# Fourier, expert and rational stages on one core: weight pairs scaled through PSUM, a sine stage that accumulates both signs, and a Nyquist row brought in by DMA

## Chip, cores and metric

The kernel runs on one core of a Trainium2 chip. The metric is device time in microseconds (us), the median of several runs. The profile is one further execution, taken with the hardware profiler.

## What is computed

The reference chains three parts. The first takes the real part of a two-dimensional Fourier transform of `x` (8 batches, 3072 x 256, float32), the second sends every one of the 24576 rows to one of eight experts, the third is a layer with a rational activation:

```python
X = np.fft.fft(x, axis=1)
X = np.fft.fft(X, axis=2)
x = X.real                                    # 24576 rows of 256
e = argmax(x @ w_gate);  g = softmax(x @ w_gate)[e]
x = g * (relu(x @ w1[e]) @ w2[e])             # w1[e] 256x1024, w2[e] 1024x256
h = x @ w_in                                  # 256x2048
g = (a0 + a1*h + a2*h**2 + a3*h**3) / (1 + |b0|*|h| + |b1|*h**2 + 1e-6)
out = g @ w_out                               # 2048x256
```

## The kernel before

The program has a Fourier part (the first eighth of the time) and an expert and rational part (the rest). The change lies in the Fourier part alone.

The Fourier part runs a loop of steps `s`, one for each batch `b` and half `jh` of the first transform's outputs: 16 steps and a last pass. Every engine takes its instructions in the order in which the loop body writes them, so the order in the body is the order on each queue. A step works on several things at once.

- **Folding** (VectorE, DVE). `fold_a`, `fold_b` and `fold_c` combine the rows of batch `b + 1` by symmetry, half of them in each step, into the operands `eo`. When `fold_c` has read its half of `xh`, SyncE (SP) issues `load_x`, 1.5 MB for the batch after (L254). That happens in steps 0 to 11, since the later steps have no further batch to load.
- **First transform** (TensorE, PE). `stage1` (L426) does one of four products of the step (even and odd, cosine and sine): three or six float32 matmuls with 384 columns into a PSUM bank of the pool `psA`. ScalarE (ACT) moves the result to the tiles `u[0]` to `u[3]`. The sine products have 127 rows, so row 127 of `u[1]` and `u[3]` is unused.
- **Second transform** (PE, ACT, DVE) of the step before. `second(p, g)` for g = 0, 1, 2 calls `stage2`, which makes two blocks of 128 rows. A block takes three matmuls of 137 columns, 129 of the transform and 8 gate logits: the cosine part (L442), the Nyquist row `u128` through a matmul with 8 rows (L443), and the sine part, which has its own columns (L445). ACT copies the cosine part to `pp` (L448), and DVE makes sum and difference into the output rows `y`, forward and mirrored, and into the logits `L` (L451 to L456).
- **Gate.** `choose` (DVE) finds the expert of a row, `gate_rank` (PE, L492 to L497) counts the rows of each expert two steps later, `gate_b` inside `finish` (DVE, L509 to L537) turns counts into addresses, and `send` scatters the rows: 12 indirect DMAs a step, issued by GpSimd (POOL, L541). `second_norm` (ACT, L484) sums squares of the rows.
- **Weight jobs.** The 16 weight matrices `w1[e]`, `w2[e]` (1 MB each, 128 x 2048 float32) become pairs of float16, a high half and the rest, scaled by a power of two, and go to `ws` in DRAM. One job runs per step, spread over two steps: `job_load` (SP, L558 and L561), `job_square` (ACT, L568), `job_sum` (PE, L572, inside `gate_rank`), `job_factor` (DVE, inside `gate_b`), `job_scale` (ACT, L589, in place), `job_split` (high half by ACT, L593; the rest by POOL, L594), `job_store` (SP, L598, one step on). A job has two buffers `wf` for the loaded matrix and two buffers `wh` for the pair. The load of the next matrix waits until L594 has read the old one.

SP's queue in a step of before is: load, store, then `load_x`. At the top of step 15 it also takes two 1 MB loads of `w_in`. All these go through the one hardware DMA queue of SP.

PSUM holds three banks for `psA`, two double banks for `psB` (`pq` of `stage2`) and one bank for everything small (`psS`).

Of the kernel before, what the change touches and what calls it, by code (L numbers as in the profile page):

```python
# [20 lines left out]
P = 128  # L21
S = 3072
# [13 lines left out]
def shape_constants():  # L36
# [23 lines left out]
    c["c_rs"] = np.sin(v * (((m[:, None] + 1) * k2[None, :]) % D)).astype(np.float32)  # L60
# [4 lines left out]
    c["c_lg"] = np.ascontiguousarray(np.concatenate([cf, sf, alt], 2)).astype(np.float32)  # L65
    r8 = np.ones((8, 145), np.float32)
    r8[:, :129] = (-1.0) ** k2
    r8[:, 137:] = np.eye(8)
# [55 lines left out]
def fourier_moe_rational_kernel(ctx, tc, xl, wg, w1, w2, w_in, w_out, av, bv, cst, out):  # L124
# [90 lines left out]
    with ExitStack() as c1:  # L215
# [23 lines left out]
        rc, rs, onesf = carve(0, 137), carve(0, 137), carve(0, P)  # L239
# [4 lines left out]
        r8 = carve(1, 145)[0:8]  # L244
# [16 lines left out]
        lg = spare[0][:, 0:528].rearrange("p (t c) -> p t c", t=2)  # L261
# [17 lines left out]
        nc.sync.dma_start(out=rs[:, 0:129], in_=cst["c_rs"])  # L279
# [83 lines left out]
        def edge_logits():  # L363

            pl = psS.tile([P, 512], F32, tag="ss", name="pl")
            for t in range(2):
                nc.tensor.matmul(pl[:, 0:8], lhsT=lg[:, t, 0:128], rhs=wgt[:, t], start=t == 0, stop=t == 1)
            for t in range(2):
                nc.tensor.matmul(pl[:, 8:16], lhsT=lg[:, t, 128:256], rhs=wgt[:, t], start=t == 0, stop=t == 1)
            for t in range(2):  # L370
                nc.tensor.matmul(pl[0:8, 16:24], lhsT=lg[:, t, 256:264], rhs=wgt[:, t], start=t == 0, stop=t == 1)
            V.tensor_copy(out=rc[:, 129:137], in_=pl[:, 0:8])
            V.tensor_copy(out=rs[:, 129:137], in_=pl[:, 8:16])
            al = fp.tile([8, 8], F32, name="al")
            V.tensor_copy(out=al, in_=pl[0:8, 16:24])
            V.tensor_tensor(out=r8[:, 129:137], in0=r8[:, 129:137], in1=al, op=ALU.mult)
# [57 lines left out]
        def stage2(b, jh, u, g, y, L, rb):  # L434

            pq = psB.tile([P, 2, 512], F32, tag="s2", name="pq")
            for k in range(2):
                par, q = divmod(2 * g + k, 3)
                ueu, uou = u[2 * par], u[2 * par + 1]
                js = slice(q * 128, q * 128 + 128)  # L440
                jg = jh * NH + q * 128
# [7 lines left out]
            La, Lm = L[:, 4 * g:4 * g + 2], L[:, 4 * g + 2:4 * g + 4]  # L449
            ya, ym = y[:, 0:2], y[:, 2:4]  # L450
            V.tensor_tensor(out=La, in0=pp[:, :, 129:137], in1=pq[:, :, 385:393], op=ALU.subtract)  # L451
            V.tensor_tensor(out=Lm, in0=pp[:, :, 129:137], in1=pq[:, :, 385:393], op=ALU.add)
            V.tensor_tensor(out=ya[:, :, 0:129], in0=pp[:, :, 0:129], in1=pq[:, :, 256:385], op=ALU.subtract)
            V.tensor_tensor(out=ym[:, :, 0:129], in0=pp[:, :, 0:129], in1=pq[:, :, 256:385], op=ALU.add)
            V.tensor_tensor(out=ya[:, :, 255:128:-1], in0=pp[:, :, 1:128], in1=pq[:, :, 257:384], op=ALU.add)
            V.tensor_tensor(out=ym[:, :, 255:128:-1], in0=pp[:, :, 1:128], in1=pq[:, :, 257:384], op=ALU.subtract)  # L456
# [29 lines left out]
        def gate_rank(key, nt, sums=()):  # L486
# [12 lines left out]
            for i, n in enumerate(sums):  # L499
                job_sum(n, pr[:, 144 + i:145 + i], start=False, skip_group_check=True)  # L500
            gst[key] += (pr,)

        def gate_b(key, ys_, nt, big, idsrc, idoff, sums=()):
# [8 lines left out]
            for i, n in enumerate(sums):  # L512
                job_factor(n, pr[:, 144 + i:145 + i])
# [57 lines left out]
        def job_sum(n, dst, **kw):  # L571
            nc.tensor.matmul(dst, lhsT=onesf, rhs=J[n][2], stop=True, **kw)  # L572

# [12 lines left out]
        def job_scale(n):  # L586
            e, which = jobs[n]
            wf = J[n][0]
# [19 lines left out]
        def job_alone(n):  # L608
            pa = psS.tile([P, 512], F32, tag="ss", name="pa")
            job_sum(n, pa[:, 0:1], start=True)  # L610
            job_factor(n, pa[:, 0:1])

# [8 lines left out]
        U, Y, LL, NQ, RB = {}, {}, {}, {}, {}  # L621

        def second(s, g):
            b, jh = steps[s]
# [6 lines left out]
            stage2(b, jh, U[s], g, y, LL[s], RB[b])  # L631

        def batch_row(b):
            RB[b] = gp.tile([8, 137], F32, tag="rb", name="rb")
            V.tensor_scalar(out=RB[b], in0=r8[:, 0:137], scalar1=r8[:, 137 + b:138 + b], scalar2=None, op0=ALU.mult)
# [7 lines left out]
        def finish(s, sums=()):  # L643
            b, jh = steps[s]
            sli, gt = gate_b(s, Y[s], 12, None if jh else bigm[:, 0:12], ids[:, jh], b * S, sums)
            top_norm(NQ.pop(s), gt, 12)
            return Y.pop(s), sli
# [39 lines left out]
        for s in range(NS + 1):  # L687
# [4 lines left out]
            for n in new:  # L692
                job_load(n)
            for n in old:
                job_store(n)
            old = now
# [3 lines left out]
            if on:  # L700
# [4 lines left out]
                if s and jh == 0:  # L705
                    batch_row(b)
                stage1(b, jh, eo, 0, u)
            if s == 0:
                stage1(b, jh, eo, 2, u)
                job_square(0)  # L710
                edge_logits()
                batch_row(0)
            if 2 <= s < NS:
                second_norm(s - 2, 2)
            if fold:
                fold_a(b + 1, jh)
            if s and s != NS - 1:
                second(p, 0)
            if 2 <= s < NS:
                gate_rank(s - 2, 12, now)  # L720
                send(*finish(s - 2, now))
# [3 lines left out]
            if s and on:  # L725
                stage1(b, jh, eo, 1, u)
            if s:
# [11 lines left out]
            for n in now:  # L739
                if s == 1:  # L740
                    job_square(n)
                    job_alone(n)
                job_scale(n)
            if s == 0:
                edge_col(0, 0)
                edge_col(0, 1)
                job_alone(0)
# [4 lines left out]
            if fold:  # L752
                fold_c(b + 1, jh, nxt)
            if s:
                second(p, 2)
                second_norm(p, 1)
                if on:
                    choose(p)
            for n in now:
                job_split(n, nc.gpsimd if s != NS - 2 else V)  # L760
            if on:
                stage1(b, jh, eo, 3, u)
            if s == NS - 1:
# [7 lines left out]
            if s == 0:  # L771
                job_scale(0)
                job_split(0)
                job_store(0)
            else:
                for n in new:
                    job_square(n)
            if on and jh == 1:
                eo = nxt
        for n in old:  # L780
            job_store(n)
# [589 lines left out]
```

## Time and profile before

| | |
|---|---|
| median of 3 runs | 3660.04 us (3654.47 to 3663.76) |
| profiled execution | 3663.37 us, of which the span from first to last instruction is 3661.3 us |
| mean granted TensorE clock | 0.978 of full speed |
| PE matmul busy over the span | 3498.4 us (96%) |
| DVE, ACT, POOL busy over the span | 3085.3, 3176.3, 3059.6 us |

The profile gives, for the one core, busy time by engine, groups of equal instructions by source line, the instructions in order of time with what ended the idle time ahead of them, and the chain of work that ended last. Times in a view count from the first instruction. The shares over the whole span are dominated by the expert and rational part, so the Fourier part has to be read from its own stretches.

### The profile page before, as it was taken

How to read it: one execution, taken by the hardware profiler on the slowest of the kernel's cores; microseconds unless marked ns; L12 is line 12 of the kernel's file. 1: busy time of each engine (PE TensorE's matmuls, PEld its weight loads, DVE VectorE, ACT ScalarE, POOL GpSimd, SP SyncE). 2: the span in 40 equal slices, each digit the busy share in tenths (PEclk: the TensorE clock that was granted, in tenths of full speed). 3: DMA queues.
4: the chain of work that ended last, by engine and by line, in shares of the span. 5: the costliest groups of instructions: out<-in, count | busy, mean ns of one | idle time of the engine just before them, and what ended most of it. 6: DMA issues, size and time to landing. Idle time of an engine off the chain costs nothing.

```text
span 3661.3 us, 76234 instructions
## 1 busy us (share of the span) xinstructions
PE 3498.4 (96%) x30136; PEld 3014.4 (82%) x30136; DVE 3085.3 (84%) x3531; ACT 3176.3 (87%) x4082; POOL 3059.6 (84%) x2874
## 2 busy tenths in 40 slices
PE   6999588999999999999999999999999999999996
PEld 3665377888888888888888888888888888888885
DVE  6888566888888888888888888888888888888887
ACT  3666346999999999999999999999999999999997
POOL 3777566888888888888888888888888888888886
PEclk9899689999999999999999999999999999999999
DMA  6666452521133111511151113222332113321210
GB/s 251 216 230 198 166 142 45 90 44 41 45 64 68 45 41 41 90 43 42 43 89 45 39 43 70 60 45 42 67 67 44 39 43 70 61 45 42 45 33 18
DMA packets 342823, 270.16 MB, mean 74 GB/s; under 512 B 180382, under 2 KB 317606, under 8 KB 335152
## 3 DMA queue, kind: packets, MB, share of 16 engines
q1 hardware_dynamic: 309440, 185.32, 20.7%
q0 software_dynamic: 33024, 79.96, 8.9%
q8 instruction: 236, 3.87, 0.6%
q14 instruction: 123, 1.01, 0.1%
HBM read 329.07 MB, written 96.92 MB: 116 GB/s over the span
## 4 chain that ended last, share of the span: by engine, by line
POOL 39%; ACT 27%; issue 14%; PE 13%; DVE 5%; DMA 1%; another core or an unknown queue 1%; POOLq 0%; SPq 0%; DVEq 0%; ACTq 0%
POOL glo L1210 12%; POOL bnd L1141 5%; POOL out_dram L1235 5%; ACT ghi L1209 5%; ACT hhi L1084 4%; PE ps L426 4%; ACT h L1198 3%; POOL wslot L856 3%; ACT L L1196 3%; POOL xr L1035 2%; PE po L1222 1%; POOL xp L1036 1%; PE h L1064 1%; PE h L1067 1%; PE pq L445 1%
## 5 line engine op out<-in xcount | busy, mean ns | idle before, releaser
L1064 PE MATMUL h<-yr,win 128*128 128x256 f16 x3072 | 753.9, 273 | 4.7 <-DVE u__48257 L1201 2.0
L1065 PE MATMUL h<-yr,win 128*128 128x256 f16 x3072 | 753.9, 273 | 0.0
L1222 PE MATMUL po<-wout,ghi 128*128 128x256 f16 x6144 | 733.6, 273 | 12.8 <-ACT ghi L1209 8.8
L1222 PEld LDWEIGHTS <-ghi 128*128 128x128 f16 x6144 | 600.5, 98 | 84.2 <-ACT ghi L1209 13.8
L1067 PE MATMUL h<-yr,win 128*128 128x256 f16 x3072 | 586.4, 273 | 0.0
L1198 ACT ACTIVATE h<-L,bnd 128x1024 f32<-128x1024 f32 x385 | 429.7, 1116 | 41.2 <-DVE u__48756 L1189 1.6
L1064 PE MATMUL h<-xt,wslot 128*128 128x256 f16 x1648 | 407.6, 274 | 12.4 <-DVE hlo L1090 5.7
L1065 PE MATMUL h<-xt,wslot 128*128 128x256 f16 x1648 | 407.8, 274 | 0.0
L1222 PE MATMUL po<-wout,glo 128*128 128x256 f16 x3072 | 398.5, 273 | 2.5 <-POOL glo L1210 2.4
L1064 PE MATMUL py<-hhi,wslot 128*128 128x256 f16 x1648 | 377.8, 276 | 6.1 <-ACT hhi L1084 4.7
L1065 PEld LDWEIGHTS <-wslot 128*128 128x128 f16 x3296 | 324.6, 98 | 71.6 <-issue 33.5
L1065 PE MATMUL py<-hhi,wslot 128*128 128x256 f16 x1648 | 377.6, 276 | 0.0
L1064 PEld LDWEIGHTS <-wslot 128*128 128x128 f16 x3296 | 324.9, 99 | 47.9 <-issue 5.9
L1067 PEld LDWEIGHTS <-wslot 128*128 128x128 f16 x3296 | 324.2, 98 | 42.3 <-issue 3.0
L1222 PEld LDWEIGHTS <-glo 128*128 128x128 bf16 x3072 | 300.1, 98 | 38.8 <-POOL glo L1210 4.1
L1065 PEld LDWEIGHTS <-win 128*128 128x128 f16 x3072 | 300.6, 98 | 38.0 <-issue 3.2
L1064 PEld LDWEIGHTS <-win 128*128 128x128 f16 x3072 | 300.6, 98 | 37.0 <-DVE u__48257 L1201 2.3
L1067 PEld LDWEIGHTS <-win 128*128 128x128 f16 x3072 | 300.6, 98 | 34.7
L1067 PE MATMUL h<-xt,wslot 128*128 128x256 f16 x1648 | 317.0, 274 | 0.0
L541 POOL DMA_INDIRECT xs<-y,sli x192 | 214.6, 1118 | 85.9 <-issue 49.5
L1090 DVE SCALAR_TENSOR_TENSOR hlo<-h,hhi 128x1024 f16<-128x1024 f32 x197 | 239.9, 1218 | 22.5 <-ACT hhi L1084 16.0
L1235 POOL DMA_INDIRECT out_dram<-o,id x192 | 199.2, 1037 | 53.0 <-issue 44.6
(4922 smaller groups left out, 9583.8 us busy)
## 6 DMA issues: line engine op xcount, KB each, us to landing
xr<-xs SPq DMA_DIRECT2D x103, 258.0 KB
ys<-yw SPq DMA_DIRECT2D x103, 256.0 KB
yr<-ys SPq DMA_DIRECT2D x96, 256.0 KB
xh<-x_l SPq DMA_DIRECT2D x14, 1536.0 KB
wf<-in_moe_w_dram SPq DMA_DIRECT2D x16, 1024.0 KB
ws<-wh SPq DMA_DIRECT2D x16, 1024.0 KB
wslot<-ws SPq DMA_DIRECT2D x4, 1024.0 KB
xh<-x_l SPq DMA_DIRECT2D x4, 768.0 KB
```

Source lines behind the costliest of these rows:

```text
L426: nc.tensor.matmul(ps[0:m, 0:n], lhsT=lhsT, rhs=mat[:, c, 0:n], start=c == 0, stop=c == nk - 1)
L541: ins = nc.gpsimd.indirect_dma_start(out=xs, out_offset=bass.IndirectOffsetOnAxis(ap=sli[:, t0 + t:t0 + t + 1], axis=0), in_=y[:, t], in_o ...
L1064: nc.tensor.matmul(ps, lhsT=wa[i], rhs=xa[i], start=i == 0, stop=False)
L1065: nc.tensor.matmul(ps, lhsT=wb[i], rhs=xa[i], start=False, stop=False)
L1067: nc.tensor.matmul(ps, lhsT=wa[i], rhs=xb[i], start=False, stop=i == n - 1)
L1090: V.scalar_tensor_tensor(out=hlo[:, sl], in0=ps, scalar=0.0, in1=hhi[:, sl], op0=ALU.max, op1=ALU.subtract)
L1141: nc.gpsimd.tensor_scalar(out=out, in0=in0, scalar1=a, scalar2=b, op0=op0, op1=op1)
L1198: nc.scalar.activation(out=ps, in_=L, func=AF.Exp, scale=-1.0, bias=st["bnd", j][3])
L1209: nc.scalar.activation(out=ghi, in_=w_, func=AF.Copy)
L1210: (V if fs[0] else nc.gpsimd).tensor_tensor(out=glo, in0=w_, in1=ghi, op=ALU.subtract)
L1222: nc.tensor.matmul(ps[:, q], lhsT=g[:, f - fs[0], q * P:(q + 1) * P], rhs=wout[:, h, 4 * u + f], start=g is ghi and u == 0 and f == 0 and ...
L1235: ins = nc.gpsimd.indirect_dma_start(out=out, out_offset=bass.IndirectOffsetOnAxis(ap=t[:, q:q + 1], axis=0), in_=o[:, q], in_offset=None, ...
```

## The change

What each engine does for a weight job is new. ACT makes the high half straight from the loaded matrix with the scale (`job_half`), and scales the matrix once more in four quarters of 512 columns, each into one PSUM bank of a new pool `psW` (`job_full`). DVE subtracts the high half from the bank (`job_rest`). POOL has no part in it any more, and the matrix is no longer overwritten. Bank `psW` is single and is also where `job_sum` puts its column, so the quarters and the sum take turns in it. `psA` gives one bank up for it.

The pieces are spread over two steps. The squares of a job move from the end of the step in which its load was issued to the top of the next step, behind `stage1(0)`. The sum moves out of `gate_rank` to behind `stage1(1)`. Half and quarter 0 come after `second(p, 1)`, quarter 1 after `second(p, 2)`, quarter 2 at the end of the step, quarter 3 in the next step behind `second(p, 0)`. The store, and behind it the load of the next matrix, move from the top of the step to behind `finish`.

In `stage2` a block takes two matmuls of 274 columns in place of three of 137: the cosine part against the constants twice over, and the sine part against minus and plus the constants, summed in PSUM. Row 127 of the sine constants holds the alternating signs of the Nyquist row, and row 127 of `u[1]` and `u[3]` gets the Nyquist row itself: `column_row` issues two DMAs of 1.5 KB (SP) at the end of each step, from `u128` into the tiles. DVE and ACT then only copy: ACT the forward part of both signs in one instruction, DVE the logits and the two mirrored parts. `batch_row` and `pp` go away.

```diff
-    c["c_rs"] = np.sin(v * (((m[:, None] + 1) * k2[None, :]) % D)).astype(np.float32)
+    rs = np.sin(v * (((m[:, None] + 1) * k2[None, :]) % D))
+    rs = np.stack([-rs, rs], 1)
+    rs[127] = (-1.0) ** k2
+    c["c_rs"] = rs.astype(np.float32)
...
-        psA = c1.enter_context(tc.tile_pool(name="psA", bufs=3, space=PSUM))
+        psA = c1.enter_context(tc.tile_pool(name="psA", bufs=2, space=PSUM))
...
+        psW = c1.enter_context(tc.tile_pool(name="psW", bufs=1, space=PSUM))
...
-        def stage2(b, jh, u, g, y, L, rb):
+        def column_row(b, jh, u):
+
+            for par in range(2):
+                nc.sync.dma_start(out=u[2 * par + 1][P - 1:P], in_=u128[b:b + 1, par, jh * NH:jh * NH + NH])
+
+        def stage2(u, g, y, L):
...
-                nc.tensor.matmul(pq[:, k, 0:137], lhsT=ueu[:, js], rhs=rc, start=True, stop=False)
-                nc.tensor.matmul(pq[:, k, 0:137], lhsT=u128[0:B, par, jg:jg + 128], rhs=rb[0:B],
-                                 start=False, stop=True)
-                nc.tensor.matmul(pq[:, k, 256:393], lhsT=uou[0:P - 1, js], rhs=rs[0:P - 1],
-                                 start=True, stop=True)
-            pp = gp.tile([P, 2, 137], F32, tag="pp", name="pp")
-            nc.scalar.activation(out=pp, in_=pq[:, :, 0:137], func=AF.Copy)
...
+                nc.tensor.matmul(pq[:, k, 0:274], lhsT=u[2 * par][:, js],
+                                 rhs=rc.unsqueeze(1).to_broadcast([P, 2, 137]), start=True, stop=False)
+                nc.tensor.matmul(pq[:, k, 0:274], lhsT=u[2 * par + 1][:, js],
+                                 rhs=rs.rearrange("p s c -> p (s c)"), start=False, stop=True)
+            p4 = pq[:, :, 0:274].rearrange("p k (s c) -> p s k c", s=2)
+            y4 = y.rearrange("p (s k) d -> p s k d", s=2)
+            nc.scalar.activation(out=y4[:, :, :, 0:129], in_=p4[:, :, :, 0:129], func=AF.Copy)
+            V.tensor_copy(out=L[:, 4 * g:4 * g + 4].rearrange("p (s k) e -> p s k e", s=2), in_=p4[:, :, :, 129:137])
+            for s_ in range(2):
+                V.tensor_copy(out=y4[:, s_, :, 255:128:-1], in_=p4[:, 1 - s_, :, 1:128])
...
+        def job_sum(n):
+
+            pw = psW.tile([P, 512], F32, tag="w", name="pw")
+            nc.tensor.matmul(pw[:, 0:1], lhsT=onesf, rhs=J[n][2], start=True, stop=True)
+            job_factor(n, pw[:, 0:1])
...
-            nc.scalar.activation(out=wf, in_=wf, func=AF.Copy, scale=(s1c, s2c)[which][:, e:e + 1])
-
-        def job_split(n, engine=nc.gpsimd):
-            wf, wh, _ = J[n]
-            nc.scalar.activation(out=wh[:, 0], in_=wf, func=AF.Copy)
-            engine.tensor_tensor(out=wh[:, 1], in0=wf, in1=wh[:, 0], op=ALU.subtract)
...
+        def job_half(n):
+            wf, wh, sc = job_scaled(n)
+            nc.scalar.activation(out=wh[:, 0], in_=wf, func=AF.Copy, scale=sc)
+
+        def job_full(n, k):
+
+            wf, _, sc = job_scaled(n)
+            pw = psW.tile([P, 512], F32, tag="w", name="pw")
+            nc.scalar.activation(out=pw, in_=wf[:, 512 * k:512 * k + 512], func=AF.Copy, scale=sc)
+            J[n].append(pw)
+
+        def job_rest(n, k):
+
+            wh, pw = J[n][1], J[n][3 + k]
+            c = slice(512 * k, 512 * k + 512)
+            V.tensor_tensor(out=wh[:, 1, c], in0=pw, in1=wh[:, 0, c], op=ALU.subtract)
```

The loop body of a step (0 < s < 15) is then, in order, with the moved or new calls marked by +:

```
  stage1(0)   + job_square(now)   second_norm(s-2, 2)   fold_a   + job_rest(old, 2)
  second(p, 0)   + job_full(old, 3)   gate_rank(s-2)   send(finish(s-2))
+ job_rest(old, 3)   + job_store(old)   + job_load(new)
  stage1(1)   + job_sum(now)   second(p, 1)   second_norm(p, 0)   fold_b
+ job_half(now)   + job_full(now, 0)   stage1(2)   fold_c with load_x   + job_rest(now, 0)
  second(p, 2)   second_norm(p, 1)   + job_full(now, 1)   choose(p)   + job_rest(now, 1)
  stage1(3)   + column_row   + job_full(now, 2)
```

In step 15 quarters 2 and 3 and the store follow at once at the end, and in step 0 job 0 does its half, its four quarters and its store there.

## Rows read from the trace of the kernel before

**Rows 1.** Busy time by stretch: busy and count for PE, PEld, DVE, ACT, POOL, then clock, DMA share, GB/s.

```profile
123.00:354.00 231.00, 212.40 (x981) 137.57 (x981) 197.89 (x569) 153.18 (x396) 179.04 (x131) 0.91 0.68 223
460.00:3661.00 3201.00, 3136.61 (x28510) 2784.83 (x28510) 2738.82 (x2514) 2926.70 (x3431) 2760.73 (x2648) 0.99 0.26 54
```

**Rows 2.** POOL in order of time: start, duration, instruction, idle time before and its end.

```profile
109.30 4.10 POOL L594 TENSOR_TENSOR wh<-wf,wh 128x2048 f16<-128x2048 f32 x1
...
222.85 4.09 POOL L594 TENSOR_TENSOR wh<-wf,wh 128x2048 f16<-128x2048 f32 x1
...
228.87 0.99 POOL L541 DMA_INDIRECT xs<-y,sli  x1 [1.94 <-DVE y L529]
...
358.89 4.08 POOL L594 TENSOR_TENSOR wh<-wf,wh 128x2048 f16<-128x2048 f32 x1
```

**Rows 3.** DVE in order of time around the same POOL instruction.

```profile
222.95 4.11 DVE L514 TENSOR_TENSOR pos<-pos,o 128x96 f32<-128x96 f32 x1
227.09 0.25 DVE L516 TENSOR_REDUCE sl<-pos 128x12 f32<-128x96 f32 x1
...
229.18 0.17 DVE L537 TENSOR_TENSOR nrm<-nq,nrm 128x12 f32<-128x12 f32 x1
```

**Rows 4.** Groups by form, 80 to 420 us: busy, mean ns, idle before and its releasers.

```profile
L541 POOL DMA_INDIRECT xs<-y,sli x173 | 194.4, 1123 | 76.3 <-issue 44.0 <-DVE y L529 27.7 <-DVE ee L329 1.5
L484 ACT ACTIVATE sq<-y 128x256 bf16<-128x256 f32 x176 | 73.1, 416 | 7.7 <-DVE y L455 3.6
...
L594 POOL TENSOR_TENSOR wh<-wf,wh 128x2048 f16<-128x2048 f32 x14 | 58.3, 4164 | 32.5 <-ACT wh L593 20.7 <-issue 11.7
...
L448 ACT ACTIVATE pp<-pq 128x274 f32<-128x274 f32 x44 | 17.3, 393 | 46.3 <-PE pq L445 32.4 <-remote 8.4 <-issue 2.9
...
L589 ACT ACTIVATE wf<-wf,s1c 128x2048 f32<-128x2048 f32 x7 | 13.9, 1987 | 0.0
...
L325 DVE TENSOR_TENSOR xh<-xh 128x384 f32<-128x384 f32 x6 | 3.3, 548 | 0.0
```

**Rows 5.** PE in order of time, the matmuls that bound steps and blocks.

```profile
81.03 0.40 PE L442 MATMUL pq<-wslot,u 128*128 128x137 f32 x2
...
242.35 0.59 PE L572 MATMUL pr<-part,wslot 128*128 128x1 f32 x2 [4.00 <-issue]
...
267.12 0.46 PE L492 MATMUL pr<-o,tri 128*128 128x88 f16 x11
...
286.25 0.46 PE L492 MATMUL pr<-o,tri 128*128 128x88 f16 x11
...
291.34 4.04 PE L426 MATMUL ps<-wslot,oo 128*128 128x384 f32 x12
295.21 0.40 PE L442 MATMUL pq<-wslot,u 128*128 128x137 f32 x2
...
297.39 3.07 PE L426 MATMUL ps<-so,oo 128*127 128x384 f32 x9
...
304.51 0.40 PE L442 MATMUL pq<-wslot,u 128*128 128x137 f32 x2
```

**Rows 6.** SP's DMA issues of one step, in order of time.

```profile
226.96 0.38 SPq L561 DMA_DIRECT2D wf<-in_moe_w_dram  x1
227.38 0.58 SPq L598 DMA_DIRECT2D ws<-wh  x1
233.54 0.32 SPq L254 DMA_DIRECT2D xh<-x_l  x1
```

**Rows 7.** Busy time in stretches of 2 us in that step, columns as in Rows 1.

```profile
234.00:236.00 2.00, 2.00 (x9) 1.24 (x7) 2.00 (x8) 1.17 (x3) 1.50 (x2) 1.00 1.13 416
...
242.00:244.00 2.00, 1.65 (x4) 1.26 (x5) 0.00 (x0) 1.94 (x9) 1.70 (x2) 0.50 0.73 272
244.00:246.00 2.00, 2.00 (x4) 1.01 (x3) 0.98 (x5) 1.12 (x6) 1.68 (x3) 0.50 0.26 91
```

**Rows 8.** Chain that ended last, behind the first loads of the expert part: start, us, what.

```profile
462.42 10.89 DMA ab<-in_moe_a_dram
```

More of the change, by code (lines that the diff above doesn't have):

```diff
@@ L64, in shape_constants @@
     alt = np.repeat(((-1.0) ** kk)[:, None], 8, 1).reshape(2, 128, 8).transpose(1, 0, 2)
-    c["c_lg"] = np.ascontiguousarray(np.concatenate([cf, sf, alt], 2)).astype(np.float32)
-    r8 = np.ones((8, 145), np.float32)
+    sa, sb = -sf, sf.copy()
+    sa[:, :, 127] = sb[:, :, 127] = alt[:, :, 0]
+    c["c_lg"] = np.ascontiguousarray(np.concatenate([cf, sa, sb, alt], 2)).astype(np.float32)
+    r8 = np.ones((8, 137), np.float32)
     r8[:, :129] = (-1.0) ** k2
-    r8[:, 137:] = np.eye(8)
     c["c_r8"] = r8
@@ L367, in edge_logits @@
                 nc.tensor.matmul(pl[:, 0:8], lhsT=lg[:, t, 0:128], rhs=wgt[:, t], start=t == 0, stop=t == 1)
+            for s_ in range(2):
+                for t in range(2):
+                    nc.tensor.matmul(pl[:, 8 + 8 * s_:16 + 8 * s_], lhsT=lg[:, t, 128 + 128 * s_:256 + 128 * s_],
+                                     rhs=wgt[:, t], start=t == 0, stop=t == 1)
             for t in range(2):
-                nc.tensor.matmul(pl[:, 8:16], lhsT=lg[:, t, 128:256], rhs=wgt[:, t], start=t == 0, stop=t == 1)
-            for t in range(2):
-                nc.tensor.matmul(pl[0:8, 16:24], lhsT=lg[:, t, 256:264], rhs=wgt[:, t], start=t == 0, stop=t == 1)
+                nc.tensor.matmul(pl[0:8, 24:32], lhsT=lg[:, t, 384:392], rhs=wgt[:, t], start=t == 0, stop=t == 1)
             V.tensor_copy(out=rc[:, 129:137], in_=pl[:, 0:8])
-            V.tensor_copy(out=rs[:, 129:137], in_=pl[:, 8:16])
+            V.tensor_copy(out=rs[:, :, 129:137], in_=pl[:, 8:24].rearrange("p (s c) -> p s c", s=2))
             al = fp.tile([8, 8], F32, name="al")
-            V.tensor_copy(out=al, in_=pl[0:8, 16:24])
+            V.tensor_copy(out=al, in_=pl[0:8, 24:32])
             V.tensor_tensor(out=r8[:, 129:137], in0=r8[:, 129:137], in1=al, op=ALU.mult)
@@ L484, in norms, with gate_rank @@
                 nc.scalar.activation(out=sq, in_=y[:, t, 0:D], func=AF.Square, accum_out=nq[:, t:t + 1])
-        def gate_rank(key, nt, sums=()):
+        def gate_rank(key, nt):
             sh, o1 = gst[key]
@@ L498, in gate_rank, with gate_b @@
                                  stop=t == nt - 1, skip_group_check=True)
-            for i, n in enumerate(sums):
-                job_sum(n, pr[:, 144 + i:145 + i], start=False, skip_group_check=True)
             gst[key] += (pr,)
-        def gate_b(key, ys_, nt, big, idsrc, idoff, sums=()):
+        def gate_b(key, ys_, nt, big, idsrc, idoff):
             sh, o1, pr = gst.pop(key)
@@ L606, in jobs_of @@
             return range(min(NJB, 1 + per * s), min(NJB, 1 + per * (s + 1)))
[L608 to L611, printed above, removed]
         edge_rows()
@@ L630, in second @@
             Y[s].append(y)
[L631 to L635, printed above, removed]
+            stage2(U[s], g, y, LL[s])
         def second_norm(s, g):
@@ L641, in choose, with finish @@
             gate_a(s, LL.pop(s), 12, None if steps[s][1] else msk[:, 0:12])
-        def finish(s, sums=()):
+        def finish(s):
             b, jh = steps[s]
-            sli, gt = gate_b(s, Y[s], 12, None if jh else bigm[:, 0:12], ids[:, jh], b * S, sums)
+            sli, gt = gate_b(s, Y[s], 12, None if jh else bigm[:, 0:12], ids[:, jh], b * S)
             top_norm(NQ.pop(s), gt, 12)
@@ L691, in fourier_moe_rational_kernel @@
             new = jobs_of(s) if on else ()
[L692 to L696, printed above, removed]
             if s == NS - 1:
@@ L704, in fourier_moe_rational_kernel @@
                 u = U[s] = {}
-                if s and jh == 0:
-                    batch_row(b)
                 stage1(b, jh, eo, 0, u)
+            for n in now:
+                job_square(n)
             if s == 0:
@@ L716, in fourier_moe_rational_kernel @@
                 fold_a(b + 1, jh)
+            for n in old:
+                job_rest(n, 2)
             if s and s != NS - 1:
                 second(p, 0)
+            for n in old:
+                job_full(n, 3)
             if 2 <= s < NS:
-                gate_rank(s - 2, 12, now)
-                send(*finish(s - 2, now))
+                gate_rank(s - 2, 12)
+                send(*finish(s - 2))
+            for n in old:
+                job_rest(n, 3)
+                job_store(n)
+            old = now
+            for n in new:
+                job_load(n)
             if s == NS - 1:
@@ L726, in fourier_moe_rational_kernel @@
                 stage1(b, jh, eo, 1, u)
+            for n in now:
+                job_sum(n)
             if s:
@@ L746, in fourier_moe_rational_kernel @@
                 edge_col(0, 1)
-                job_alone(0)
+                job_sum(0)
             if s == 2:
@@ L753, in fourier_moe_rational_kernel @@
                 fold_c(b + 1, jh, nxt)
+            for n in now:
+                job_rest(n, 0)
             if s:
@@ L756, in fourier_moe_rational_kernel @@
                 second_norm(p, 1)
+                for n in now:
+                    job_full(n, 1)
                 if on:
@@ L759, in fourier_moe_rational_kernel @@
             for n in now:
-                job_split(n, nc.gpsimd if s != NS - 2 else V)
+                job_rest(n, 1)
             if on:
                 stage1(b, jh, eo, 3, u)
+                column_row(b, jh, u)
+            for n in now:
+                job_full(n, 2)
+                if s == NS - 1:
+                    job_rest(n, 2)
+                    job_full(n, 3)
+                    job_rest(n, 3)
+                    job_store(n)
+                    old = ()
             if s == NS - 1:
@@ L771, in fourier_moe_rational_kernel @@
             if s == 0:
-                job_scale(0)
-                job_split(0)
+                job_half(0)
+                for k in range(4):
+                    job_full(0, k)
+                    job_rest(0, k)
                 job_store(0)
-            else:
-                for n in new:
-                    job_square(n)
             if on and jh == 1:
                 eo = nxt
-        for n in old:
-            job_store(n)
         p = NS - 1
```

38 lines of the change are left out of this document (11 added, 27 removed).

## Prediction

> **What bounds the kernel now.** I read busy time by stretch first. From 460 us on nothing is touched by the change, and PE is busy 3136.61 of 3201 us there, so that part is taken as fixed [rows 1]. The steps of the Fourier part lie in 123 to 354 us. There PE is busy 92% at a granted clock of 0.91, DVE 86%, POOL 78% and ACT 66% [rows 1]: no engine is full, so the limit is a loop of waits, and the order in time has to show which.
>
> POOL shows it. Its weight instruction L594 starts at 109.30 and, eleven steps on, at 358.89, which is 22.69 us a step, and nowhere between does POOL wait ahead of L594 [rows 2]. A step of POOL is L594 (4.1), then a wait of 1.9 for DVE's write of the rows' gate [rows 2], then twelve scatters of 1.12 with about 0.3 of issue between them [rows 4]: 4.1 + 1.9 + 13.4 + 3.3 = 22.7. The wait closes the loop: L514 on DVE starts 0.1 us behind L594 and takes 4.11 where L516, on as many elements, takes 0.25, and it ends when L594 ends; the address chain follows, and only then may POOL scatter [rows 2, 3]. So **POOL bounds these steps**, by itself and by what it holds up in DVE. PE with no gap does a step in 286.25 - 267.12 = 19.1 us [rows 5]. Between the first second-stage matmul of step 2 (81.03) and that of step 12 (304.51) lie ten steps of 22.35 us on average [rows 5]; this is what the new loops are compared with.
>
> **The change part by part.**
>
> *POOL.* L594 goes, and with it the stall of L514. POOL is left with 13.4 + 3.3 = 17 us of scatters and whatever it waits for. If nothing else came up the next bound would be PE.
>
> *PE.* Two blocks of the second stage take 297.39 - 295.21 = 2.18 us, 1.09 a block and 0.36 for a matmul of 137 columns; six matmuls of 384 columns take 295.21 - 291.34 = 3.87, so 0.645 each [rows 5]. A matmul of 274 columns was not run. By columns from the wide one it is 0.46, by a line through both sizes 0.52; I take 0.5, so a block of 1.0 and 0.5 us off a step (six blocks). At the ends of 0.36 and 0.645 it would be 2.2 off or 1.2 on. PE's step at full clock becomes 18.6.
>
> *ACT.* Scale (1.99 [rows 4]) and the plain high half go, the scaled high half costs about the same as one of them, and four quarters come. A quarter lies between the 256 columns of L484 (0.42) and a quarter-share of L589 (0.50) on one side and the straight line between L484 and L589 on the other, 0.64 [rows 4]; I take 0.64. The copy of 516 elements in place of 274 (0.39 [rows 4]) adds 0.2 three times a step. Together about +1.2 on some 15 us busy a step (153.18 over ten steps [rows 1]). That is off the path while ACT has 5 us free in a step.
>
> *DVE.* A quarter's subtraction lies between 0.55 (384 elements [rows 4]) and twice that by size, I take 0.65, 2.6 a step. Against that stand the 3.9 of L514 [rows 3] where POOL was over it, and four additions per `second` that become three copies. DVE's total falls from 19.8 (197.89 over ten steps) to some 18. It is hidden behind a step of over 20, and would be the bound only below that.
>
> *The bank `psW`.* `job_sum` on PE needs the bank that `job_rest(old, 3)` empties, and that subtraction stands on DVE behind the whole of `finish`. From the end of `gate_rank` DVE needs 0.6 for the two reads of the counts, 0.25 for L514 without POOL, 229.35 - 227.09 = 2.26 for L516 to L537 [rows 3], and 0.65 for the quarter: 3.8. PE meanwhile has only `stage1(1)`, three matmuls or 1.9 us. So PE waits 1.9 with `second(p, 1)` and the rest of the step queued behind it, a loop of 18.6 + 1.9 = 20.5. A gap has a second price: behind the 4.00 us gap at 242.35 [rows 5] the clock granted was 0.50 [rows 7]. Nothing to 1.5 us of that gives 20.5 to 22, and I take 21.
>
> *The Nyquist row.* This is the part that I think decides. `column_row` is SP's last issue of a step, behind the store (1 MB), the load (1 MB) and `load_x` (1.5 MB), and `second(p, 0)` needs the row of `u[1]` two microseconds of `stage1(0)` later. Before, the same three transfers were issued at 226.96, 227.38 and 233.54 [rows 6]; the DMA share was full at 234 (1.13, 416 GB/s), still 0.73 in 242 to 244 and 0.26 in 244 to 246 [rows 7]. So the last of them was through about 16.5 us after the first issue, with 15 and 18 as ends. A small transfer does not pass large ones on this queue: the 2 KB of `ab` landed 10.89 us after its issue behind the expert part's first weight loads [rows 8]. The loop is then: the row lands; PE finishes `second(p, 0)` and `gate_rank` in 1.5 + 0.9; `finish` and quarter 3 take the 3.8 above less 0.4 that overlaps; SP issues store and load, 5.8 us after the row; the three transfers take 16.5; the next row comes about 0.7 behind. `load_x` is not the late one in this, since `fold_c` comes some 6 us behind the store's issue, as far as before (6.6 [rows 6]). **The step is 5.8 + 16.5 + 0.7 = 23.0**, between 21.5 and 24.5 by the ends of the transfers. If PE comes out of its wait at half clock, the first 2.4 us take twice as long and the step is 25.4. I take 23.5, nearer the first, since a slow PE waits less. Steps 2 to 11 have all three transfers: ten times 23.5 - 22.35 = +11.5. In steps 12 to 14 there is no `load_x`, the row comes early, and the loop of 21 counts against 22.7: three times -1.7 = -5.
>
> The Trainium skill, page "DMA: Bandwidth & Descriptors", section "Queues, rings and completion order", says that each DMA engine takes its ring's descriptors in order, but that a later transfer on few engines may complete ahead of an earlier one's other engines. The 10.89 us of [rows 8] agree with the first half; which ring a row takes no row here shows. If it took the one that is done first, the loop would go by the short end, 21.5, and the sum by -9.
>
> *Ends.* In step 0 job 0 runs its quarters alone through one bank: four times 0.64 + 0.65 on ACT and DVE in turn, and a half of 2.0, 7.2 where ACT had 3.9. Between 0 and 3.3 of it comes on top; I take 2. In step 15 the last two quarters (2.6) stand ahead of the gate, where before L594 stood over L514 for some 3: nothing, within 3 either way. The bank that `psA` loses costs nothing as long as a `second` lies between two products, which gives ACT 2 us for a product's copy; without that cover it would be up to 0.9 a product.
>
> *Sum.* 11.5 - 5 + 2 = +8.5 on the profiled execution's 3663.4, so 3672. That execution lies 3.3 above the median shown; for the median it is 3660 + 8.5, **3669 us**.
>
> **Rivals.**
>
> *A, the forecast:* the row behind the three transfers takes POOL's place at 23 to 24 us a step. For it speaks that all of the loop is in order on one queue each. Against it, that 16.5 is read from shares of a queue and not from the landing itself. It gives 3650 to 3685.
>
> *B, faster: the row is early enough.* If the transfers are through 2.5 us sooner after the store, the bank loop decides everywhere: thirteen steps at 21 in place of 22.4 are -19, and with the 2 of step 0 the time is 3643 (3633 at 20.2 a step, with blocks by columns alone). What speaks for it is the queue's free time before (share 0.68 on average [rows 1]) and the rule cited above. It decides as soon as the row lands less than 21 us after the last one.
>
> *C, slower: the clock falls with each wait.* The wait for the row comes in every step, at one place, right ahead of the work on which the store depends; at half clock the step is 25.4, ten times +3 = +31, -5 + 2, so 3688, and up to 3700 if `stage1(1)` and the sum are slow too. The 0.50 behind the gap [rows 7] speaks for it; against it, that a PE that is slow reaches the row later and so waits less.
>
> *D, nothing freed:* POOL stays the bound. Its 17 us are below every other loop, so this would need scatters that wait for something else; 3660.
>
> **How the numbers follow.** Two runs of this kernel differ by about 0.3% (11 us), so closer times count as the same. A has 0.45, B 0.29, C 0.2, D 0.06. Faster than 3649: most of B (0.27) and the low end of A (0.06), 0.33. Slower than 3671: all but a little of C (0.18) and the upper part of A (0.14), 0.32. The same: 0.35. The range goes from B's low end to the middle of C's span, 3632 to 3695; A's own is 3650 to 3685.
>
> **What would show it.** POOL: no instruction but scatters in the steps, with idle time ahead of the first of a step, ended by DVE. DVE: L514's successor at 0.25. PE: in steps 2 to 12 a wait of 2 to 5 us ahead of the sine matmul of `second(p, 0)`, ended by the row's DMA, gone from step 13 on; a smaller one ahead of `job_sum`, ended by DVE; blocks at 1.0. If PE's wait for the row is under 1 us, B holds; if the clock stays at 0.5 past `gate_rank` in most steps, C does. The prediction is wrong in its ground if the step is set by ACT or DVE, or if the time moves outside the Fourier part.

## The result, and the profile after

The changed kernel takes 3711.7 us (3709.9 to 3714.2, four runs) against 3660.4 us of the kernel before in the same session: a ratio of 1.0141, interval 1.0129 to 1.0153. It is **51 us slower**, above the range of 3632 to 3695. The profiled execution has a span of 3712.4 us, 51.1 more than before.

Busy time by stretch, columns as in [rows 1]:

```profile
123.00:354.00 231.00, 177.41 (x717) 114.16 (x716) 151.72 (x431) 137.84 (x359) 111.26 (x103) 0.90 0.63 199
511.00:3712.00 3201.00, 3140.72 (x28510) 2787.47 (x28510) 2738.85 (x2515) 2925.81 (x3431) 2756.41 (x2648) 0.99 0.26 54
```

The expert part has the same length and busy times as in [rows 1], only 51 us later: all of the loss lies in the Fourier part. There PE, DVE, ACT and POOL are each less busy than before: no engine has too much to do, every one waits more. PE in order of time:

```profile
82.56 0.63 PE L454 MATMUL pq<-wslot,u 128*128 128x274 f32 x2
...
349.53 0.63 PE L454 MATMUL pq<-wslot,u 128*128 128x274 f32 x2
355.14 1.23 PE L456 MATMUL pq<-rs,u 128*128 128x274 f32 x2 [4.99 <-DMA u<-u]
...
390.40 0.56 PE L589 MATMUL pw<-part,wslot 128*128 128x1 f32 x2 [7.44 <-DVE wh L611]
390.82 1.26 PE L454 MATMUL pq<-wslot,u 128*128 128x274 f32 x2
```

The first two rows are the first second-stage matmul of step 2 and of step 12, as in [rows 5]: ten steps of 26.70 us, where they were 22.35. So the 51.1 divide into +1.5 up to step 2 (82.56 - 81.03), +43.5 in the ten steps, and the remaining +6.1 behind step 12. The other rows show the two waits of PE: for the Nyquist row, and at `job_sum` for the quarter's subtraction of the job before. The waits from 123 to 354 us (total, times, longest):

```profile
POOL xs L544 <- issue: 80.7, 93, 11.5
DVE L L461 <- ACT y L460: 56.9, 16, 5.8
...
ACT u L407 <- remote: 29.5, 6, 5.5
...
PE pq L456 <- DMA u<-u: 25.4, 8, 4.0
PE pw L589 <- DVE wh L611: 24.3, 8, 5.9
```

A step here is 27.37 us: the stores of steps 3 and 12 are issued at 117.05 and 363.38, nine steps apart. All steps of runs below are taken between the same two stores. A step of PE is then 21.0 busy (177.41 / 231 x 27.37), 3.0 waiting for the row and 2.9 at `job_sum`, and 0.5 else. PE's 21.0 against the 18.6 that the prediction has at full clock is put down to the half clock behind the waits: a matmul of 274 columns takes 0.46 us, but 0.9 to 1.1 behind 390.82, where the granted clock is 0.50 (390.8 to 394.5), the lower of the two levels, 1.2 GHz. The experiment on the clock below tests this price. POOL, the bound of before, is idle 6.0 to 11.6 us ahead of the first scatter of a step.

SP's issues of one step:

```profile
335.76 0.35 SPq L615 DMA_DIRECT2D ws<-wh  x1
336.20 0.39 SPq L561 DMA_DIRECT2D wf<-in_moe_w_dram  x1
343.39 0.33 SPq L261 DMA_DIRECT2D xh<-x_l  x1
343.81 1.31 SPq L446 DMA_DIRECT2D u<-u  x2
363.38 0.35 SPq L615 DMA_DIRECT2D ws<-wh  x1
```

The row for which PE waits until 355.14 comes 19.4 us behind the store, and the next store comes 8.2 behind the row. This is the prediction's loop, with 17.2 and 5.8 in it there.

### The profile page after: what moved, and what is told of

Read it like the earlier page. It is cut to its first block, busy times and chain, and to the rows that moved or that the text cites. A ratio compares the mean times of both kernels' runs of the same rounds, so it can differ in the third digit from the quotient of the medians.

```text
span 3712.4 us, 75983 instructions
## 1 busy us (share of the span) xinstructions
PE 3490.0 (94%) x29948; PEld 3009.4 (81%) x29948; DVE 3052.7 (82%) x3442; ACT 3194.3 (86%) x4130; POOL 2983.5 (80%) x2859
## 4 chain that ended last, share of the span: by engine, by line
POOL 30%; ACT 23%; PE 17%; DVE 14%; issue 13%; DMA 2%; another core or an unknown queue 1%; SPq 0%; POOLq 0%; ACTq 0%; DVEq 0%
POOL glo L1231 9%; POOL out_dram L1256 5%; ACT ghi L1230 4%; ACT h L1219 4%; PE po L1243 3%; ACT hhi L1105 3%; POOL wslot L877 3%; DVE h L1221 3%; POOL bnd L1162 3%; PE ps L435 2%; ACT L L1217 2%; POOL xr L1056 2%; PE h L1085 2%; PE h L1088 2%; PE h L1086 2%
## 5 line engine op out<-in xcount | busy, mean ns | idle before, releaser
L544 POOL DMA_INDIRECT xs<-y,sli x192 | 205.3, 1069 | 268.2 <-issue 153.3
```

The lines of the kernel that those rows point to most:

```text
L544: ins = nc.gpsimd.indirect_dma_start(out=xs, out_offset=bass.IndirectOffsetOnAxis(ap=sli[:, t0 + t:t0 + t + 1], axis=0), in_=y[:, t], in_o ...
```

## The experiments

Theory R is the prediction's (the row sets the step). Theory Q: the bank of the quarters sets it, through DVE's order and ACT's. Theory C: the half clock behind a wait has a price of its own. All ratios are to the kernel before, run beside them (3646.8 to 3648.1 us there). The changed kernel was run in the first session alone, where the kernel before took 3660.4 us. So what an edit is worth against it is a difference of two ratios, each with its own interval, and times in the expectations are on the first session's base; the last section says what else differs in that session.

**The row first.** In `stage1` the tile is allocated ahead; then

```diff
                 u = U[s] = {}
+                if s > 1:
+                    column_row(b, jh, u)
                 stage1(b, jh, eo, 0, u)
...
                 stage1(b, jh, eo, 3, u)
-                column_row(b, jh, u)
+                if s <= 1:
+                    column_row(b, jh, u)
```

> The Nyquist row's two DMAs are issued at the start of their step, ahead of the step's store, load and load_x, instead of behind them. Theory R (the prediction's: the row behind three transfers sets the step): PE's waits for the row (32.0 us in ten) go, the step falls from some 27.5 us to the loop of the PSUM bank, 21 by the prediction; ten steps of -6.5, so about 3647. Theory Q (what sets the step is the order on ACT, square and norms ahead of the copy of the step's first second-stage block, and the bank that job_sum shares with the quarters): the wait for the row was slack in front of another wait, the steps stay at 26 to 27.5 and PE's wait at job_sum grows by what the row's loses; 3695 to 3712. Theory C (the clock falls with the row's wait): -2 us a step, some 3690.

Measured 1.0108 (1.0091 to 1.0125), which is 3700 us on the first session's base, inside Q's range, and a step of 25.88. No wait for the row is left, and the one at `job_sum` has grown. The stretch from 123 to 354 us, the wait in it, and one step in order of time (line numbers are 3 higher here):

```profile
123.00:354.00 231.00, 185.54 (x772) 122.84 (x771) 158.50 (x460) 145.91 (x380) 113.90 (x107) 0.89 0.63 203
```

```profile
PE pw L592 <- DVE wh L614: 45.5, 9, 5.3
```

```profile
264.18 1.90 ACT L574 ACTIVATE wh<-wf 128x2048 f16<-128x2048 f32 x1
...
265.79 0.45 PE L507 MATMUL pr<-o,tri 128*128 128x8 f16 x12
...
266.10 2.18 PE L435 MATMUL ps<-se,ee 128*127 128x384 f32 x6
...
267.68 0.42 ACT L494 ACTIVATE sq<-y 128x256 bf16<-128x256 f32 x1
...
268.09 0.58 ACT L463 ACTIVATE y<-pq 128x516 f32<-128x516 f32 x1
...
268.70 0.19 DVE L464 COPY L<-pq 128x32 f32<-128x32 f32 x1 [2.77 <-ACT y L463]
268.88 0.75 DVE L466 COPY y<-pq 128x254 f32<-128x254 f32 x2
269.55 0.25 DVE L517 TENSOR_TENSOR pos<-pr,run 128x96 f32<-128x96 f32 x1
...
272.16 0.68 DVE L614 TENSOR_TENSOR wh<-pw,wh 128x512 f16<-128x512 f32 x1
...
272.99 0.56 PE L592 MATMUL pw<-part,wslot 128*128 128x1 f32 x2 [4.71 <-DVE wh L614]
```

R falls as the sole cause: with the row gone from the path a step is still 25.9. This run shows the bank's loop alone. `gate_rank` ends at 266.10, the quarter's subtraction ends 6.7 us later, and `job_sum` starts 6.9 us later. PE had finished the block of `second(p, 0)` before `gate_rank`, but ACT copies it out only at 268.09, behind the job's square and four norm squares, and DVE's copies, `finish` and the quarter follow one behind the other.

**ACT's order.** `job_square` and `second_norm` of the third block go to the end of the step before:

```diff
-            for n in now:
-                job_square(n)
...
-            if 2 <= s < NS:
-                second_norm(s - 2, 2)
...
                 job_full(n, 2)
+                if s < NS - 1:
+                    second_norm(p, 2)
...
+            for n in new:
+                job_square(n)
```

> job_square goes back to the end of the step before, and the four norm squares of the third block too, so that on ACT nothing but a stage-one copy stands ahead of the copy of the first second-stage block. The row stays where it is. R: no change, the row comes as before, 3705 to 3716. Q: DVE's wait for that copy (78.9 us in 23) falls by about 4 us a step, the last quarter's subtraction and the store come up to 4 us earlier, steps 12 to 14 fall from 26.5 to about 23, the others to where the row holds them (23 to 25); -30 to -60, so 3650 to 3680.

Measured 1.0075 (1.0058 to 1.0092), a step of 24.98: about 24 us better than the change, on Q's side but less than its 30 to 60, since the row (30.8 us of waits in the Fourier part) and `job_sum` (33.9) still hold PE.

**The sum in the gate's bank.**

```diff
-            pw = psW.tile([P, 512], F32, tag="w", name="pw")
+            pj = psS.tile([P, 512], F32, tag="ss", name="pj")
```

> job_sum writes a column of the gate's bank in place of the bank of the quarters, so that PE need not wait for the last quarter's subtraction of the job before. R: PE's waits at job_sum go (42.2 us in twelve), but the wait for the row takes their place, so no change: 3700 to 3715. Q: PE gets ahead by 2 to 7 us a step and the step becomes that of the chain of quarters or of the row: -15 to -45, 3667 to 3697.

Measured 1.0010 (1.0000 to 1.0019): 48 us better than the change, 3 more than Q's range. The steps with `load_x` now take 23.84, those without 20.5 (stores at 329.05 and 390.59, three steps). PE's waits for the row in two steps, and the stores:

```profile
226.52 1.28 PE L456 MATMUL pq<-rs,u 128*128 128x274 f32 x2 [5.50 <-DMA u<-u]
...
250.34 0.73 PE L456 MATMUL pq<-rs,u 128*128 128x274 f32 x2 [3.01 <-DMA u<-u]
```

```profile
209.16 0.35 SPq L615 DMA_DIRECT2D ws<-wh  x1
...
234.71 0.35 SPq L615 DMA_DIRECT2D ws<-wh  x1
...
256.88 0.35 SPq L615 DMA_DIRECT2D ws<-wh  x1
```

Store to row takes 17.4 and 15.6, row to store 8.2 and 6.5. In these steps ACT copies the block as soon as PE has done it, so its order is not in this loop. So with the bank's loop out of the way the row does set the step, at nearly the 23.5 that the prediction gave it.

**All three.**

> All three edits: the row first, squares and norms at the end of the step before, job_sum in the gate's bank. R: as the row alone, about 3647. Q: neither wait is left, the step is that of PE with small gaps or of ACT (some 19 to 22.5 us): 3610 to 3650, below the kernel before.

Measured 0.9906 (0.9890 to 0.9923), a step of 20.70. The three single edits are worth 0.33%, 0.66% and 1.31%, 2.30% together; this run is 2.35% below the change, in Q's range. So the three costs add, as far as intervals of 0.17% on each ratio can tell.

**The quarter ahead of `finish`.** In the changed kernel alone:

```diff
             for n in old:
                 job_full(n, 3)
+                job_rest(n, 3)
+                job_store(n)
             if 2 <= s < NS:
                 gate_rank(s - 2, 12)
                 send(*finish(s - 2))
-            for n in old:
-                job_rest(n, 3)
-                job_store(n)
```

> The changed kernel with the last quarter's subtraction and the store ahead of finish on DVE and SP, not behind it; all else as changed. If the chain of finish on DVE (2.3 to 2.7 us) lies inside the loop that sets the step, both by the bank (PE's job_sum waits for that subtraction) and by the store ahead of the row, each of 14 steps gets 2 us shorter: -25 to -35, a ratio of 1.004 to 1.008 to the kernel before, where the changed one stands at 1.014. If the loop runs over PE and ACT elsewhere, the ratio stays at 1.012 to 1.015.

Measured 0.9943 (0.9926 to 0.9960): faster than the kernel before, by an edit that moves one subtraction and one store some 2.6 us forward. A step fell by 6.2 us, to 21.15; 2 was expected, and the ratio is below both ranges. Its stretch:

```profile
123.00:354.00 231.00, 205.59 (x940) 134.67 (x939) 183.62 (x552) 179.56 (x462) 151.52 (x131) 0.98 0.70 236
```

PE is busy 18.8 us of a step (205.59 / 231 x 21.15), 2.2 less than in the changed kernel, because the clock is 0.98 where it was 0.90. The wait at `job_sum` is 4.8 us in the whole stretch, 0.4 a step where it was 2.9; the row's is 20.5, 1.9 where it was 3.0. Together 5.8 of the 6.2. The moved piece lay in both loops, and with shorter waits the clock stays higher.

**Each half of the change alone.** First the weights' part, with the second stage of before; then the second stage's part, with the weights as before and the row as SP's last issue.

> Only the weights' part of the change (quarters through the bank, job_sum later, nothing by POOL), with the second stage of the kernel before, so that no Nyquist row is on a queue. By the prediction's sum the bank's loop is 21 us a step: thirteen steps of -1.4, so a ratio of 0.995 to 0.997. By Q the bank's loop is as slow as in the changed kernel's steps without load_x, 26 to 27 us: thirteen steps of +4, a ratio of 1.010 to 1.016.

Measured 1.0206 (1.0189 to 1.0223), a step of 28.16: slower than with both parts, and outside both expectations. PE waits 41.2 us at `job_sum` from 123 to 354, 5.0 a step, as with the row first; but it is busy 23.1 of a step (189.80 / 231 x 28.16) where a clean step took 19.1 [rows 5], at a clock of 0.84 against 0.89 with the row first.

> Only the second stage's part (both signs in PSUM, the row by DMA as the step's last issue), with the weights' pairs as before: scale and split by ACT and POOL, sums in the gate. By the prediction's sum the row sets 23 to 23.5 us a step in ten steps against POOL's 22.4: +6 to +12, a ratio of 1.002 to 1.003. By Q, POOL's loop goes on setting the step, less a little where DVE's copies are shorter: 0.997 to 1.001.

Measured 1.0010 (1.0000 to 1.0020): a step of 23.33 (stores at 135.07 and 321.72, eight steps), 23.03 in the kernel before (135.20 and 319.44). The ratio is at the top of Q's range, and the prediction's lies inside its interval, so the ratio cannot tell the two apart. The trace can: PE waits 36.1 us for the row in 123 to 354, but POOL never waits ahead of its weight instruction there, so POOL's loop still sets the step. So the whole loss is the weights' part; on top of it the new second stage gives 0.65% back.

**A later sum.** The three edits, with `job_sum` moved behind `second(p, 1)`:

```diff
-            for n in now:
-                job_sum(n)
             if s:
                 second(p, 1)
+            for n in now:
+                job_sum(n)
+            if s:
                 second_norm(p, 0)
```

> The three edits together (0.9906 of the kernel before, 20.8 us a step) with job_sum one block later on PE, behind second(p, 1), so that PE has the block's 1.9 us to do in place of its wait for the gate's bank (2.2 us, and half clock after it). If that wait and its half clock are what is left over PE's 19 us, a step falls by 1 to 2 us: a ratio of 0.984 to 0.988. If the chain of the four quarters, which starts with this sum, sets the step, the ratio stays at 0.990 or goes up to 0.995.

Measured **0.9884** (0.9867 to 0.9900), a step of 19.89: the lowest ratio of all, 42 us below the kernel before, just outside the range of 0.984 to 0.988. PE is busy 218.03 of 231 us, and its wait for the gate's bank is still there, 12.3 us from 123 to 354 where the three edits had 13.7. The interval overlaps that of the three edits, so the gain of this last move is not shown.

**Other combinations.** First the quarter ahead of `finish`, the row first and ACT's order; then all edits.

> The last quarter's subtraction and the store ahead of finish (0.9943 alone, 20.9 us a step), the Nyquist row first and squares and norms at the end of the step before; job_sum stays in the bank of the quarters. If the loops of bank and row are both gone, PE's 18.6 us are left with small gaps: 19 to 20 us a step, fourteen steps of -1 to -2 against 20.9, a ratio of 0.985 to 0.990. If another order on ACT or DVE sets 20.9, the ratio stays at 0.992 to 0.995.

> All edits: last quarter and store ahead of finish, row first, squares and norms at the end of the step before, job_sum in the gate's bank and behind second(p, 1). The best so far, with job_sum moved, was at 0.9884 with 18.4 and 20.8 us in turn. If the quarter behind finish still costs there, 0.983 to 0.987; if PE and the chain of quarters are level by then, 0.987 to 0.990.

Measured 0.9925 (0.9909 to 0.9942), 20.78 a step, and 0.9898 (0.9881 to 0.9915), 20.20, which cannot be told from the 0.9884. In the first, the row and ACT's order add nothing that can be told once the quarter is early: the row's wait is gone, but PE waits 20.1 us for the bank at `job_sum` from 123 to 354. In the second, PE waits there 13.9 us, which the profile puts down to ACT's squares. At 244.66 `job_sum` follows DVE's last read of the gate's bank, and DVE had waited for ACT's copy of the block, behind the squares of the norms and the job. So here the costs do not add.

**The clock.** The kernel with the row first, with matmuls into unused columns of the gate's bank ahead of `job_sum`; ten, then six:

```diff
+            if 2 <= s < NS:
+                for i in range(10):
+                    nc.tensor.matmul(warm[0][:, 256:512], lhsT=ident, rhs=so_w, start=True, stop=True,
+                                     skip_group_check=True)
             for n in now:
                 job_sum(n)
```

> The kernel with the row first (1.0108, 25.9 us a step, PE waits 4.7 us at job_sum and then runs at half clock) with ten matmuls of 256 columns put into that wait, 4.3 us of PE's work that nobody reads, so that PE is not idle ahead of job_sum. Theory C in this form (half clock behind a wait is a price of its own, some 2.2 us a step by PE's busy time of 20.8 against 18.6): the step falls to 23.5 to 24.2, a ratio of 1.000 to 1.005. If the wait alone counts, since a slow PE only waits less later: 1.009 to 1.013.

> The same with six such matmuls in place of ten: ten ran 4.4 us and held job_sum back 1.5 us longer than the bank (the quarter's subtraction ended 1.6 us before it), so a step of 25.5 could not show the price of the clock. Six end with the bank's release. If half clock behind the wait is a price of its own, the step is 23.5 to 24.2 and the ratio 1.000 to 1.005; if a slow PE only waits less later, 25.5 to 26 and 1.008 to 1.013.

Ten gave 1.0108 (1.0091 to 1.0125), six 1.0046 (1.0029 to 1.0063), with steps of 25.47 and 23.93 against 25.88 without. The run of six:

```profile
255.85 2.86 PE L748 MATMUL pr<-se,ident 128*128 128x256 f32 x12 [1.78 <-DVE run L521]
258.80 0.35 PE L594 MATMUL pw<-part,wslot 128*128 128x1 f32 x2
259.02 0.71 PE L457 MATMUL pq<-wslot,u 128*128 128x274 f32 x2
259.56 0.62 PE L459 MATMUL pq<-rs,u 128*128 128x274 f32 x2
```

Behind `job_sum` the matmuls follow at 0.46 to 0.55, where they took 0.9 to 1.05 with the wait empty, at a granted clock of 0.50 (273 to 277 us of the run with the row first). From 123 to 354 us the clock is 0.96 on average, and 0.89 without the six. The wait and the six together take as long as the empty wait did (4.9 and 5.1 us a step), so the gain is the clock's. Work that nobody reads makes the kernel 0.62% faster, some 2 us a step. Ten of them kept the clock too (0.97), but held `job_sum` back 1.5 us. The Trainium skill, page "TensorE: Matmul & The Clock Gate", section "HAM oscillation — how this bites in real kernels", says that a loop whose wait lets the clock fall pays for that in every pass, and not once. The run of six beside the one without agrees, at 2 us a pass.

## Why the prediction was wrong

**Right.** POOL was the bound and was freed: no instruction but scatters, with 6.0 to 11.6 us of idle time ahead of them. The stall of [rows 3] is gone (0.25 at L517). The prices held, as matmuls back to back and groups of the stretch from 123 to 354 show:

```profile
342.33 0.62 PE L456 MATMUL pq<-rs,u 128*128 128x274 f32 x2
342.79 0.62 PE L454 MATMUL pq<-wslot,u 128*128 128x274 f32 x2
343.25 0.62 PE L456 MATMUL pq<-rs,u 128*128 128x274 f32 x2
```

```profile
L611 DVE TENSOR_TENSOR wh<-pw,wh 128x512 f16<-128x512 f32 x35 | 24.0, 687 | 9.2 <-ACT pw L604 8.5 <-issue 0.5
L604 ACT ACTIVATE pw<-wf,s2c 128x512 f32<-128x512 f32 x19 | 12.9, 678 | 0.0
```

A matmul of 274 columns, taken at 0.5, follows the last at 0.46. 0.64 for ACT's quarter was 0.68, 0.65 for DVE's was 0.69, and PE's step at full clock, 18.6, was 18.8 where little is waited for. What lies ahead of step 2 cost 1.5, 2 was taken for step 0. The bank that `psA` lost cost nothing that shows: PE waits for a copy of a product at most 1.2 us from 123 to 354 in any run. No size of an instruction explains the miss.

**The step that failed is the bank `psW`**: "From the end of `gate_rank` DVE needs ... 3.8. ... So PE waits 1.9", and 21 us a step. The run with the row first has 6.7, a wait of 4.7 in the step shown and 5.1 on average (45.5 / 231 x 25.88), and 25.9. Two things were left out. DVE's copies of `second(p, 0)`, 0.85 us, stand ahead of `finish`. They wait for ACT's copy, which stands behind the square and the norms, 3.9 us of ACT's queue: "off the path while ACT has 5 us free in a step" counted ACT's time and not its order. `finish` starts 3.45 us behind `gate_rank` for these two (269.55), and it and the quarter then take 3.3. A third was sized too small: the half clock was taken as 0.5 where it is 2.2, which is PE's 20.8 busy (185.54 / 231 x 25.88) less 18.6; the six matmuls won 2 of it back. So the step is 18.6 + 5.1 + 2.2 = 25.9.

ACT's order could have been read before. In that trace the squares and norms lay in front of the same copy already; the block was done on PE at some 214.8:

```profile
215.32 1.91 ACT L568 ACTIVATE wh<-wf 128x2048 f16<-128x2048 f32 x1 [3.81 <-issue]
...
217.98 0.42 ACT L484 ACTIVATE sq<-y 128x256 bf16<-128x256 f32 x1
...
220.02 0.38 ACT L448 ACTIVATE pp<-pq 128x274 f32<-128x274 f32 x1
```

There DVE stood behind POOL next, and nobody waited for `finish` but the scatters; what the order cost there was not tried. The change put PE behind `finish`.

**The row** was sized well and judged wrongly. It was to decide, at 23.5 us a step; with the bank out of the way it does, at 23.84. That the two are so near is in part luck: row to store was taken as 5.8 and takes 8.2 and 6.5, store to row as 17.2 and takes 17.4 and 15.6. In the changed kernel taking the row away gives 0.33%. The sign named for it did come, ten waits of PE for the row in steps 3 to 12, 1.6 to 5.0 us each, and none behind; such a wait shows that the row is late, and not that it alone sets the step. The two loops are coupled: `fold_c` on DVE waits behind PE's `second(p, 1)`, so a late `job_sum` makes `load_x` late (7.6 us behind the store, against 5.1 with the sum's own bank), and the row behind it. The prediction had ruled that out ("`load_x` is not the late one in this"). This turns 17.2 into 19.4, and the half clock and the copies of the block by ACT and DVE turn 5.8 into 8.2. The ten steps came to +43.5 for the +11.5 of the sum. The row of 1.5 KB came 11.3 us behind its issue at 343.81, behind the transfers ahead of it. This agrees with the half of the Trainium skill's rule (page "DMA: Bandwidth & Descriptors", section "Queues, rings and completion order") that the prediction kept.

**Behind step 12** there was to be a gain of 5; it is a loss of 6. Without `load_x` the bank's loop holds: 26.3 us a step (stores at 363.38 and 442.19, three steps), where 21 was taken. Three steps of +3.6 against 22.7 would be +11, so the end gives some 5 back, for which nothing, within 3, was taken; what gives it back stays open. With the sum's own bank a step is 20.5.

**Rivals.** B (21 a step) needed the same bank's loop and fell with it. D did not occur. C came nearest, with the price right (2.4 us for its one wait, 2.2 measured) and the place half right: the clock falls at `job_sum` too. It stopped at 3700 because it left the 21 behind step 12 untouched: the 11 us from -5 to +6 there are what it lacks. Its +43 for the ten steps is near the +43.5 by luck in part, since it has the row's wait alone where there were two.

## What to carry to other kernels

A buffer that engines share in turns makes the whole queue in front of each turn part of the loop: write the loop out with every instruction that stands ahead of its members on their engines, not only the members. Free time on an engine says nothing of its order. When TensorE waits in every pass and the trace shows the clock low behind the wait, add the half-clock work; and try first to move the instruction that releases the buffer forward, which here was worth about 72 us for one edit.

## Not expected of the hardware, and open

Six matmuls that nobody reads, in a wait of PE, saved some 2 us a step.

In the changed kernel ACT also stands 5.4 us ahead of one copy in every second step, with no releaser that the profile names:

```profile
133.85 0.43 ACT L407 ACTIVATE u<-ps,wslot 127x192 f32<-127x192 f32 x1 [5.45 <-remote]
...
135.74 0.62 PE L456 MATMUL pq<-rs,u 128*128 128x274 f32 x2
135.83 1.93 ACT L571 ACTIVATE wh<-wf 128x2048 f16<-128x2048 f32 x1
...
139.78 0.58 ACT L460 ACTIVATE y<-pq 128x516 f32<-128x516 f32 x1
```

Five of these end 9.0 to 9.2 us behind the issue of `load_x` (124.67 for this one), and the chain that ended last runs through all five:

```profile
128.40 5.43 another core or an unknown queue
```

They cost time here. The squares start late behind the stall, and the copy of the block, done on PE at 136.4, waits until 139.78. By that measure the five hold the copy back 3.4, 2.6, 2.4, 1.2 and 0.1 us, an estimate of some 10 of the 43.5 us. In the other steps with `load_x` the copy comes within 0.7 us of PE's end, so that there ACT's order costs next to nothing.

The kernel before has such stalls too in that session (4.3 and 5.3 us at the same copy, at 338.29 and 390.10, and 2.9 and 8.4 at others), and none of the twelve later traces has one. What ends them was not tried and stays open, and so does whether they go with the session or with the kernel. So the row's 0.33% (12 us), and part of the 0.66% of ACT's order, may be what these stalls cost and not what the edits won. The bank's loop does not hang on them: the runs with the row first and with the weights' part alone lose 1.08% and 2.06% without one.

It stays open too why the clock is lower with the weights' part alone (0.84) than with the row first (0.89), at the same wait.
